# All products of y in 32-wide tiles, and the products for the carried state behind them in the same slot

## The chip, the cores and the metric

The kernel runs on one core of one Trainium2 chip. The metric is the device time of one execution in microseconds (us); lower is better. Engines are named as the profile names them: PE does the matmuls, PEld loads their weights, DVE, ACT and POOL do the elementwise work, SP issues the DMAs.

## The reference

Three stages follow one another: a gated linear attention over 4 batches of 8 heads, 768 positions and 48 features, then two MLPs over the 3072 tokens.

```
f = 1 / (1 + exp(-f_logit))
for t in range(S):
    state = f[:, :, t, :, None] * state + einsum('bhd,bhe->bhde', k[t], v[t])
    y[t]  = einsum('bhd,bhde->bhe', q[t], state)
x = y as (3072, 384)
x = (h * cos(h)) @ w_out,  h = x @ w_in                      # 384 -> 2048 -> 384
x = rmsnorm(x); out = (silu(x @ w_gate) * (x @ w_val)) @ w_out2
```

## The kernel before

**Steps and pieces.** The attention is done in 24 steps, each of which is one chunk of 128 positions of one batch (6 steps to a batch) and all 8 heads. Heads stand in 4 pairs i, with the two heads j of a pair at partitions 0 and 64. Within a step the product of q and k is masked and multiplied with v (the part inside the chunk), and q is multiplied with the state that the chunks before left (the carried part; the first step of a batch has none). A step's PE work is written in four pieces, `piece_pe(n, p)`:

- p = 0: transposes of the scaled k (`tr`), line 350 (not in the last step of a batch)
- p = 1: products of k and q for the two heads of each pair (`sc`), line 359
- p = 2: `zs(n)`, line 382: the products of k and v that are added to the carried state, 8 matmuls 64 columns wide with 48 columns moving (not in the last step of a batch)
- p = 3: `ys(n)`: the products that make y, in one PSUM bank of 128 x 384. For each of two groups c of heads there are two 64-wide matmuls of the carried state `Tz` with q (line 400) and four 32-wide ones of v with the masked product `am` (line 406). They cover 32 of the 48 features of each head. The 16 others follow 32 wide: four with `Tz` (line 412) and eight with the tile `vtl` (line 418).

Each of these calls is an fp32 matmul, and the trace shows each as two matmuls, so that line 382 has 16 in a step. "Wide" is the number of columns of weights, and so of output partitions; narrow matmuls that write different partitions can run beside each other.

**Slots.** Steps 0 to 3 run in a prologue (`PROLOGUE`). From then on the pieces are dealt out one to a slot, and a slot is one tile of 128 of the first MLP's 2048 hidden features for one block of 512 tokens: there are 6 blocks of 16 slots. On PE a slot is `H` (9 matmuls, line 606), then the piece `P`, then `m1_out` of the slot two before (9 matmuls, line 657). The string `SLOT` (first block, middle blocks, last block) gives the order in which the engines' instructions are written; every engine works through its own in that order. What DVE, ACT and POOL do for a piece is written one slot later, in the slot whose `p0` is that piece's number:

- p0 = 0: `kn` (ACT copies the transposed k out of PSUM), `ff`, `grd` and `scan` (the gates of the next step: a scan on DVE whose end values POOL copies to `pall`)
- p0 = 1: `am` (mask of the product), second `scan`
- p0 = 2: `st` (`state`, line 462: DVE adds the products of `zs` to the state), `kt` (k of the next step scaled)
- p0 = 3: `xh` and `xl` (y split into two parts by ACT and DVE), `qt` (q of the next step scaled), `cy` (`carry`, lines 325 and 331: the state times the chunk's decay, on DVE and into `Tz` on POOL)

For the MLP each slot has `k` (ACT, line 615), `w` (DVE, line 621), `s` (ACT, line 627), `g` (DVE, line 632), and for the slot before it `hi` (ACT, line 640) and `lo` (POOL, line 647, tile `gl`). On POOL, the copy to `pall` is written ahead of `lo`. In the third slot of a block ACT also empties the three accumulators of the block before (line 669), and `m1_out` waits for it; that slot always holds a piece p = 3 (steps 8, 12, 16 and 20).

**Banks.** From step 4 on the PSUM banks of the pieces come in turn from three (`att_bank`): `tr` one, `sc` two, `zs` one, `ys` one. `FLIP` is 10: up to step 9 PE transposes f, k and q of the next step behind the pieces (`turn1`, line 231), from step 10 on DVE does it.

Of the kernel before, what the change touches and what calls it, by code (L numbers as in the profile page):

```python
# [28 lines left out]

SLOT = (  # L30
# [3 lines left out]
)  # L34
SLOT2 = (
# [14 lines left out]
def kernel(  # L50
# [14 lines left out]
    nc = tc.nc  # L65
    B, H, S, D = q.shape
# [3 lines left out]
    C = 128  # L70
# [48 lines left out]
    xh = [pp.tile([128, KD, 512], F32R, name=f"xh{i}") for i in range(2)]  # L119
    xl = [pp.tile([128, KD, 512], F32R, name=f"xl{i}") for i in range(2)]  # L120
# [4 lines left out]
    FLIP = 10  # L125
# [4 lines left out]
    am = [ap_.tile([128, 512], F32, name=f"am{i}") for i in range(2)]  # L130
    vtl = [ap_.tile([128, NP, 3, 16], F32, name=f"vtl{i}") for i in range(2)]
# [38 lines left out]
    st = {}  # L170
# [174 lines left out]
    def piece_pe(n, p):  # L345
        if p == 0:
            if not last(n):
                t = st[n, "tr"] = att_bank()
                for i in range(NP):
                    nc.tensor.transpose(t[:, 128 * i:128 * (i + 1)], st[n, "kt"][:, i, :], ident)  # L350
            if n >= HEAD and n + 1 < NSTEP:
                turn1(n + 1, 0)
                load_v(n + 1)
        elif p == 1:
            t = [att_bank(), att_bank()]
            for i in range(NP):
                for j in range(2):
                    o = 64 * j
                    nc.tensor.matmul(  # L359
                        t[j][:, C * i:C * (i + 1)], st[n, "kt"][o:o + D, i, :],  # L360
                        st[n, "qt"][o:o + D, i, :], start=True, stop=True,
                    )
            st.pop((n, "kt"))
            st[n, "sc"] = t
        elif p == 2:
            zs(n)
            if n >= HEAD and n + 1 < NSTEP:
                turn1(n + 1, 1)
        else:
            ys(n)  # L370
            if n >= HEAD and n + 1 < NSTEP:
                turn1(n + 1, 2)

    def zs(n):
        if last(n):
            return
        t = att_bank()
        kn = st.pop((n, "kn"))
        for i in range(NP):
            for j in range(2):  # L380
                o = 64 * j
                nc.tensor.matmul(
                    t[o:o + 64, D * i:D * (i + 1)], kn[:, 128 * i + o:128 * i + o + 64],
                    st[n, "v"][:, 2 * i + j, :], start=True, stop=True,
                )
        st[n, "z"] = t

    def ys(n):
        if True:
            t = att_bank()  # L390
            qt, vt, vt2 = st.pop((n, "qt")), st.pop((n, "v")), vtl[n % 2]
            inter = n % NCH > 0


            for c in range(2):
                cs = slice(C * c, C * (c + 1))
                if inter:
                    for x in range(2):
                        i = 2 * c + x
                        nc.tensor.matmul(  # L400
                            t[64 * x:64 * x + 64, cs], Tz[:, i, 0:64], qt[:, i, :],
                            start=True, stop=False,
                        )
                for x in range(4):
                    i, j = divmod(4 * c + x, 2)
                    nc.tensor.matmul(  # L406
                        t[32 * x:32 * x + 32, cs], vt[:, 2 * i + j, 0:32],
                        am[j][:, C * i:C * (i + 1)], start=not inter, stop=True,
                    )
            if inter:  # L410
                for i in range(NP):
                    nc.tensor.matmul(
                        t[32 * i:32 * i + 32, 2 * C:3 * C], Tz[:, i, 64:96], qt[:, i, :],
                        start=True, stop=False,
                    )
            for j in range(2):
                for i in range(NP):
                    nc.tensor.matmul(  # L418
                        t[32 * i:32 * i + 32, 2 * C:3 * C], vt2[:, i, j:j + 2, :],
                        am[j][:, C * i:C * (i + 1)],  # L420
                        start=not inter and j == 0, stop=j == 1,
                    )
            st[n, "y"] = t
# [413 lines left out]
    if True:  # L837
# [120 lines left out]
        for j, (t0, N) in enumerate(blocks):  # L958
            final = j == len(blocks) - 1
            if final:  # L960
                assert not pieces and prev is None
                att.close()
                p2 = stack2.enter_context(tc.tile_pool(name="p2", bufs=1))
                for x in range(4):
                    free2.append(tuple(
                        p2.tile([128, DM], F32R, name=f"xunit{2 * x + y}") for y in range(2)
                    ))
                for i in range(N1):
                    free2 += [wi[i], wo[i]]
                order2 = [(nm, i) for i in range(N2) for nm in ("g", "v", "o")]  # L970
                for u, key in enumerate(order2):
                    w2[key] = free2[u]
                dec2 = Decode([
                    (w_out2_w, 128 * i, None, lambda nm=nm, i=i: w2[nm, i]) if nm == "o"
                    else (w_gate_w if nm == "g" else w_val_w, None, 128 * i,
                          lambda nm=nm, i=i: w2[nm, i])
                    for nm, i in order2
                ], 1)
                norm(0, slot + 8)
            for i in range(N1):  # L980
                cur = pieces.pop(0) if pieces else None
                n0, p0 = prev or (0, -1)
                more = n0 + 1 < NSTEP
                env = dict(d=dec if j == 0 else dec2)
                do = {
                    "H": lambda: m1_h(j, i),
                    "pe": lambda: run(pe_at, slot),
                    "hi": lambda: gp and m1_hi(*gp),
                    "lo": lambda: gp and m1_lo(*gp),
                    "kn": lambda: p0 == 0 and not last(n0) and kn_evac(n0),  # L990
                    "tanh": lambda: p0 == 0 and n0 + 1 < FLIP and gates(n0 + 1),
                    "ff": lambda: p0 == 0 and more and flip_f(n0 + 1),
                    "grd": lambda: p0 == 0 and more and (
                        guard_f(n0 + 1), n0 + 1 >= FLIP and gates(n0 + 1)
                    ),
                    "scan": lambda: more and (
                        p0 == 0 and scan_end(n0 + 1) or p0 == 1 and scan_start(n0 + 1)
                    ),
                    "am": lambda: p0 == 1 and causal(n0),
                    "st": lambda: p0 == 2 and state(n0),  # L1000
                    "kt": lambda: p0 == 2 and more and scale_k(n0 + 1),
                    "qt": lambda: p0 == 3 and more and scale_q(n0 + 1),
                    "xh": lambda: p0 == 3 and x_hi(n0),
                    "xl": lambda: p0 == 3 and x_lo(n0),
                    "cy": lambda: p0 == 3 and more and carry(n0 + 1),
                    "act": lambda: run(act_at, slot),
                    "k": lambda: env.update(k=m1_k(j, i)),
                    "w": lambda: env.update(w=m1_w(j, i, env["k"])),
                    "s": lambda: m1_cos(j, i, env["w"]),
                    "dv": lambda: run(dve_at, slot),  # L1010
                    "g": lambda: env.update(g=m1_g(j, i, env["w"])),
                    "t": lambda: env["d"] and env["d"].step_split(),
                    "x": lambda: env["d"] and env["d"].step_x(),
                    "f": lambda: env["d"] and env["d"].step_f(),
                    "po": lambda: run(post_at, slot),
                    "P": lambda: cur and piece_pe(*cur),
                }
                for key in SLOT[0 if j == 0 else 2 if final else 1].split():
                    do[key]()
                gp = j, i, env["g"]  # L1020
                prev = cur
                outs.append((j, i))
                if len(outs) > 2:
                    m1_out(*outs.pop(0))
                slot += 1
            finish(j, slot, final)
# [285 lines left out]
```

## Time and profile before

| | |
|---|---|
| median of 3 runs | 1039.61 us (1038.75 to 1039.67) |
| the profiled execution | 1038.93 us, of which the trace spans 1037.2 us |
| PE busy in the span | 996.0 us (96%) |
| DVE, ACT, POOL busy | 622.0 us (60%), 418.9 us (40%), 324.4 us (31%) |
| instructions | 15616, 5920 of them matmuls |

Times of the trace are counted from the start of the span. A matmul's row gives its start and a modelled duration; matmuls overlap, so the distance from one start to the next says what one costs.

### The profile page before, as it was taken

The numbers are of one execution on the slowest core, as the hardware profiler recorded it, in microseconds if no ns is written. First come the engines' busy times: TensorE is split into PE (matmuls) and PEld (weight loads), VectorE is DVE, ScalarE is ACT, GpSimd is POOL, SyncE is SP. The second block draws the span as 40 slices with busy tenths as digits, with TensorE's granted clock in tenths as the row PEclk, the third lists the DMA queues.
The fourth block names the chain that finished last, engine by engine and source line by source line (L and its number), as shares of the span: only waits on it lengthen the run. The fifth ranks groups of instructions, "written<-read, shape, count | busy, mean of one in ns | idle before, by whom it ended". The sixth has DMA issues, their size and how long they took to land.

```text
span 1037.2 us, 15616 instructions
## 1 busy us (share of the span) xinstructions
PE 996.0 (96%) x5920; PEld 812.7 (78%) x5920; DVE 622.0 (60%) x946; ACT 418.9 (40%) x737; POOL 324.4 (31%) x374
## 2 busy tenths in 40 slices
PE   6788899999999999999999999999999999999997
PEld 5556677777777777777777788888888888888886
DVE  7888875777777777776478676335335335335222
ACT  2466655444445444453677544212212222222111
POOL 1555653532532444344388353001001001001000
PEclk9799999999999999999999999999999999999999
DMA  8875222222223222321243443342343343332000
GB/s 172 193 186 134 80 59 71 60 50 66 80 65 71 81 56 59 93 46 9 91 132 93 145 148 107 92 132 87 112 132 92 110 141 95 122 117 61 31 1 34
DMA packets 123855, 96.10 MB, mean 93 GB/s; under 512 B 69238, under 2 KB 103030, under 8 KB 123772
## 3 DMA queue, kind: packets, MB, share of 16 engines
q1 hardware_dynamic: 123772, 95.03, 33.8%
q8 instruction: 48, 0.79, 0.3%
q14 instruction: 35, 0.29, 0.1%
HBM read 85.54 MB, written 9.46 MB: 92 GB/s over the span
## 4 chain that ended last, share of the span: by engine, by line
PE 80%; DVE 9%; ACT 4%; issue 2%; DMA 2%; POOL 2%; SPq 1%; DVEq 0%; ACTq 0%; POOLq 0%
PE bank L759 29%; PE bank L657 16%; PE bank L795 15%; PE bank L606 13%; DVE E L284 1%; PE bank L359 1%; PE bank L406 1%; DVE wrap L621 1%; PE bank L400 1%; DVE g L632 1%; PE bank L418 1%; DVE wx L562 1%; DMA nat<-in_k_dram 1%; DVE ft L293 1%; ACT wrap L627 1%
## 5 line engine op out<-in xcount | busy, mean ns | idle before, releaser
L657 PE MATMUL bank<-gh,wo 128*128 128x512 f32 x576 | 207.4, 414 | 4.4 <-ACT x L669 4.3
L773 DVE SCALAR_TENSOR_TENSOR u<-bank,sg 128x512 f32<-128x512 f32 x72 | 49.7, 691 | 199.4 <-PE bank L759 199.4
L647 POOL TENSOR_TENSOR gl<-g,gh 128x512 fp32r<-128x512 f32 x96 | 126.6, 1319 | 87.6 <-ACT gh L640 86.4
L657 PEld LDWEIGHTS bank<-gh,wo 128*128 128x128 f32 x576 | 109.2, 190 | 34.0 <-ACT x L669 5.4
L759 PE MATMUL bank<-xh,wo 128*128 128x512 f32 x360 | 122.8, 395 | 0.0
L657 PE MATMUL bank<-gl,wo 128*128 128x512 f32 x288 | 115.8, 402 | 6.5 <-POOL gl L647 6.4
L768 ACT ACTIVATE sg<-bank 128x512 f32<-128x512 f32 x72 | 43.0, 597 | 173.3 <-PE bank L759 173.3
L743 POOL TENSOR_TENSOR xl<-x2b,xh 128x512 fp32r<-128x512 f32 x18 | 24.2, 1344 | 283.1 <-ACT xh L742 283.1
L780 ACT CAST uh<-u 128x512 fp32r<-128x512 f32 x72 | 44.8, 622 | 151.1 <-DVE u L773 150.9
L627 ACT ACTIVATE wrap<-wrap,cb 128x512 f32<-128x512 f32 x96 | 69.3, 722 | 88.1 <-DVE wrap L621 87.4
L640 ACT CAST gh<-g 128x512 fp32r<-128x512 f32 x96 | 59.6, 620 | 106.4 <-DVE g L632 71.9
L632 DVE SCALAR_TENSOR_TENSOR g<-bank,wrap 128x512 f32<-128x512 f32 x96 | 65.6, 683 | 43.3 <-ACT wrap L627 41.5
L621 DVE SCALAR_TENSOR_TENSOR wrap<-bank,kint 128x512 f32<-128x512 f32 x96 | 65.8, 685 | 35.1 <-ACT kint L615 34.5
L615 ACT ACTIVATE kint<-bank,cb 128x512 int32<-128x512 f32 x96 | 65.9, 686 | 43.6 <-PE bank L606 43.3
L786 DVE TENSOR_TENSOR ul<-u,uh 128x512 fp32r<-128x512 f32 x72 | 51.5, 716 | 48.9 <-ACT uh L780 48.9
L759 PEld LDWEIGHTS bank<-xh,wo 128*128 128x128 f32 x360 | 67.6, 188 | 14.6
L795 PE MATMUL bank<-wo,uh 128*128 128x384 f32 x288 | 74.1, 338 | 0.0
L657 PEld LDWEIGHTS bank<-gl,wo 128*128 128x128 f32 x288 | 54.7, 190 | 21.4 <-POOL gl L647 10.2
L759 PE MATMUL bank<-xl,wo 128*128 128x512 f32 x180 | 71.0, 394 | 0.0
L795 PEld LDWEIGHTS bank<-wo,uh 128*128 128x128 f32 x288 | 52.7, 188 | 3.5 <-issue 0.5
L581 POOL TENSOR_TENSOR wo<-wx,wo 128x384 fp32r<-128x384 f32 x32 | 36.0, 1124 | 52.4 <-ACT wo L580 50.1
L490 DVE SCALAR_TENSOR_TENSOR wacc<-stage,wacc 128x384 int32<-128x384 int32 x68 | 50.8, 748 | 0.7
(343 smaller groups left out, 2196.9 us busy)
## 6 DMA issues: line engine op xcount, KB each, us to landing
stage<-in_moe_w_out_dram SPq DMA_DIRECT2D x56, 384.0 KB, 3.3
stage<-in_moe_w_gate_dram SPq DMA_DIRECT2D x24, 384.0 KB, 3.3
stage<-in_moe_w_val_dram SPq DMA_DIRECT2D x24, 384.0 KB, 3.3
stage<-in_moe_w_in_dram SPq DMA_DIRECT2D x16, 384.0 KB, 3.4
nat<-in_f_logit_dram SPq DMA_DIRECT2D x48, 96.0 KB, 2.2
nat<-in_k_dram SPq DMA_DIRECT2D x48, 96.0 KB, 2.3
nat<-in_q_dram SPq DMA_DIRECT2D x48, 96.0 KB, 2.2
v_sb<-in_v_dram SPq DMA_DIRECT2D x24, 192.0 KB, 3.6
```

What stands on the lines that cost most here:

```text
L490: nc.vector.scalar_tensor_tensor(out=wacc, in0=hi, scalar=1 << 30, in1=wacc, op0=ALU.bitwise_xor, op1=ALU.bitwise_and,)
L606: nc.tensor.matmul(t, l[:, 128 * kk:128 * (kk + 1)], r[:, kk, 0:N], start=idx == 0, stop=idx == 3 * KD - 1,)
L615: nc.scalar.activation(out=kt, in_=hb[j, i], func=AF.Identity, scale=INV2PI * UNIT, bias=cb[:, 0:1])
L621: nc.vector.scalar_tensor_tensor(out=w, in0=hb[j, i], scalar=INV2PI * UNIT, in1=kt, op0=ALU.mult, op1=ALU.subtract)
L627: nc.scalar.activation(out=w, in_=w, func=AF.Sin, scale=2.0 * math.pi, bias=cb[:, 1:2])
L632: nc.vector.scalar_tensor_tensor(out=g, in0=hb.pop((j, i)), scalar=UNIT, in1=w, op0=ALU.mult, op1=ALU.mult)
L640: nc.scalar.copy(out=h, in_=g)
L647: nc.gpsimd.tensor_tensor(out=l, in0=g, in1=h.bitcast(F32), op=ALU.subtract)
L657: nc.tensor.matmul(acc[m][:, 0:N], lw[:, cs], r, start=i == 0 and x == 0, stop=i == N1 - 1 and x == 2,)
L759: nc.tensor.matmul(t[y], l[:, 128 * kk:128 * (kk + 1)], r[:, kk, :], start=idx == 0, stop=idx == 3 * KD - 1,)
L786: nc.vector.tensor_tensor(out=l, in0=u, in1=h.bitcast(F32), op=ALU.subtract)
L795: nc.tensor.matmul(o2[tt][:, 0:DM], lu[:, cs], r, start=i == 0 and x == 0, stop=i == N2 - 1 and x == 2,)
```

## The change

In `ys`, the 64-wide matmuls with `Tz` become twice as many 32-wide ones, so that all of `ys` is 32 wide. For the steps from 9 on, `zs` moves from piece 2 to piece 3, behind `ys`, and is made of 16 matmuls 32 wide in place of 8 that are 64 wide; `state` moves with it to the slot whose `p0` is 3. In the second string of `SLOT`, `st` is written ahead of `kt`, `xh`, `xl`, `qt` and `cy`.

```
-    "tanh hi H kn ff kt xh xl qt cy am st P k w grd scan s lo act dv g pe po",
+    "tanh hi H kn ff st kt xh xl qt cy am P k w grd scan s lo act dv g pe po",
...
         elif p == 2:
-            zs(n)
+            if n + 1 < FLIP:
+                zs(n)
             if n >= HEAD and n + 1 < NSTEP:
                 turn1(n + 1, 1)
         else:
             ys(n)
+            if n + 1 >= FLIP:
+                zs(n)
...
+        M = 64 if n + 1 < FLIP else 32
         for i in range(NP):
-            for j in range(2):
-                o = 64 * j
+            for o in range(0, 128, M):
                 nc.tensor.matmul(
-                    t[o:o + 64, D * i:D * (i + 1)], kn[:, 128 * i + o:128 * i + o + 64],
-                    st[n, "v"][:, 2 * i + j, :], start=True, stop=True,
+                    t[o:o + M, D * i:D * (i + 1)], kn[:, 128 * i + o:128 * i + o + M],
+                    st[n, "v"][:, 2 * i + o // 64, :], start=True, stop=True,
                 )
...
             for c in range(2):
                 cs = slice(C * c, C * (c + 1))
-                if inter:
-                    for x in range(2):
-                        i = 2 * c + x
+                for part in (0, 1) if inter else (1,):
+                    for x in range(4):
+                        i, j = divmod(4 * c + x, 2)
                         nc.tensor.matmul(
-                            t[64 * x:64 * x + 64, cs], Tz[:, i, 0:64], qt[:, i, :],
-                            start=True, stop=False,
+                            t[32 * x:32 * x + 32, cs],
+                            vt[:, 2 * i + j, 0:32] if part else Tz[:, i, 32 * j:32 * j + 32],
+                            am[j][:, C * i:C * (i + 1)] if part else qt[:, i, :],
+                            start=part == 0 or not inter, stop=part == 1,
                         )
-                for x in range(4):
-                    i, j = divmod(4 * c + x, 2)
-                    nc.tensor.matmul(
-                        t[32 * x:32 * x + 32, cs], vt[:, 2 * i + j, 0:32],
-                        am[j][:, C * i:C * (i + 1)], start=not inter, stop=True,
-                    )
...
-                    "st": lambda: p0 == 2 and state(n0),
+                    "st": lambda: p0 >= 2 and state(n0),
```

## Rows read from the trace of the kernel before

**Rows 1.** The page: busy time, share of the span and instructions of each engine.

```profile
PE 996.0 (96%) x5920; PEld 812.7 (78%) x5920; DVE 622.0 (60%) x946; ACT 418.9 (40%) x737; POOL 324.4 (31%) x374
```

**Rows 2.** PE's waits from 160 to 500 us: total us, times, longest.

```profile
PE bank L657 <- ACT x L669: 4.3, 3, 2.0
```

**Rows 3.** Windows, one slot each: length; PE, PEld, DVE, ACT, POOL busy (instructions); clock; DMA.

```profile
226.33:230.70 4.37, 4.37 (x20) 3.30 (x19) 4.26 (x8) 1.68 (x3) 2.98 (x4) 1.00 0.13 17
488.79:492.96 4.17, 4.17 (x19) 3.38 (x18) 1.99 (x4) 1.70 (x3) 1.29 (x1) 1.00 0.44 21
315.04:320.00 4.96, 4.96 (x36) 3.85 (x34) 4.85 (x8) 1.93 (x3) 2.97 (x4) 1.00 0.03 1
320.00:326.48 6.48, 6.48 (x68) 4.67 (x66) 4.84 (x7) 2.03 (x3) 2.65 (x5) 1.00 0.28 58
```

**Rows 4.** Timeline of PE across `ys` of step 14: start, length, line, count.

```profile
300.67 0.44 PE L400 MATMUL bank<-qt,Tz 128*64 128x128 f32 x4
301.04 0.43 PE L406 MATMUL bank<-am,v_sb 128*32 128x128 f32 x8
301.40 0.44 PE L400 MATMUL bank<-qt,Tz 128*64 128x128 f32 x4
...
302.01 0.40 PE L412 MATMUL bank<-qt,Tz 128*32 128x128 f32 x8
302.23 0.62 PE L418 MATMUL bank<-am,vtl 128*32 128x128 f32 x16
302.78 0.50 PE L657 MATMUL bank<-gh,wo 128*128 128x512 f32 x1
```

**Rows 5.** `zs` of step 14 by line: duration ns min/median/max, first and last start.

```profile
L382 PE MATMUL bank<-v_sb,kn x16: 222/222/257, 295.7 to 296.1; 128*64 128x48 f32 x16
```

**Rows 6.** Timeline of DVE after `ys` of step 14.

```profile
306.21 0.56 DVE L438 TENSOR_TENSOR xl<-bank,xh 128x384 fp32r<-128x384 f32 x1 [2.23 <-ACT xh L433]
```

**Rows 7.** Timeline, slots with piece 2 of steps 11 and 15.

```profile
227.38 1.29 POOL L647 TENSOR_TENSOR gl<-g,gh 128x512 fp32r<-128x512 f32 x1
...
228.40 0.40 PE L657 MATMUL bank<-gh,wo 128*128 128x512 f32 x1
...
314.71 1.23 DVE L284 TENSOR_TENSOR_SCAN E<-ft,c 128x516 f32<-128x516 f32 x1
...
316.16 1.29 POOL L647 TENSOR_TENSOR gl<-g,gh 128x512 fp32r<-128x512 f32 x1
...
317.80 0.50 PE L657 MATMUL bank<-gh,wo 128*128 128x512 f32 x1
```

**Rows 8.** Timeline, third slot of a block (piece 3 of step 16).

```profile
344.77 0.34 DVE L462 TENSOR_TENSOR Sn<-Sn,bank 128x192 f32<-128x192 f32 x1
...
345.03 0.67 DVE L621 SCALAR_TENSOR_TENSOR wrap<-bank,kint 128x512 f32<-128x512 f32 x1
...
346.37 1.06 ACT L669 ACTIVATE x<-bank 128x512 f32<-128x512 f32 x2
...
347.00 0.50 PE L657 MATMUL bank<-gh,wo 128*128 128x512 f32 x1 [1.17 <-ACT x L669]
```

**Rows 9.** Windows right after that slot of step 12, and in the prologue.

```profile
258.10:261.50 3.40, 3.40 (x10) 2.64 (x9) 0.00 (x0) 0.65 (x2) 0.00 (x0) 0.50 0.59 231
...
26.00:32.80 6.80, 4.25 (x51) 2.74 (x52) 6.16 (x14) 1.11 (x2) 4.08 (x6) 0.50 0.85 185
```

**Rows 10.** The chain that ended last, in order of time, in the prologue.

```profile
28.55 0.69 PE bank L400 x4
...
45.49 1.25 PE bank L406 x8
```

**Rows 11.** PE's own queue: waits it passed, by line (`ys` of step 6; step 14).

```profile
117.54 0.64 PE L406 MATMUL bank<-am,v_sb 128*32 128x128 f32 x16
...
L231 PEldq EVENT_SEMAPHORE  x1: 51/51/51, 117.8 to 117.8; - x1
...
L382 PEldq EVENT_SEMAPHORE  x1: 51/51/51, 291.5 to 291.5; - x1
```

More of the change, by code (lines that the diff above doesn't have):

```diff
@@ L390, in ys @@
             t = att_bank()
-            qt, vt, vt2 = st.pop((n, "qt")), st.pop((n, "v")), vtl[n % 2]
+            qt, vt, vt2 = st.pop((n, "qt")), st[n, "v"], vtl[n % 2]
             inter = n % NCH > 0
```

## The prediction

> **What bounds the kernel now.** I read the page first: PE is busy for 996 of the span's 1037.2 us [rows 1]. That share alone says little, since a busy PE can be waiting inside a matmul, so I went on to PE's waits. From 160 us on, where steps 8 to 23 run, almost all that PE waits for is the emptying of the accumulators, 4.3 us in three slots [rows 2]; until then the first block's slots are ended by waits on DVE, ACT and POOL. Then I cut the middle blocks into slots. A slot without a piece takes 4.17 us; one with piece 2 takes 4.96, one with piece 3 takes 6.48, and PE is busy in all of each [rows 3]. The two pieces thus cost 0.79 and 2.31 us, and what they lose the kernel loses, as long as nobody else comes late.
>
> **Part 1: all of `ys` 32 wide.** I read `ys` of step 14 by the starts of its groups [rows 4]. Four 32-wide matmuls run side by side: in the middle of a 32-wide stretch 8 matmuls, two groups of four, take 302.23 - 302.01 = 0.22 us, 0.109 a group. A 64-wide stretch, two groups of two, takes 0.37 (300.67 to 301.04), and the 32-wide stretch between two 64-wide ones takes 0.36 for its two groups, so that 0.36 - 0.22 = 0.14 is the price of beginning and ending a stretch. Now: 2.11 us from 300.67 to 302.78, in four stretches. After: 14 groups in one stretch, 14 x 0.109 + 0.14 = 1.67. The gain is 0.44 us for a step with a carried part. The 4 more matmuls (8 in the trace) that the step gets are in the 14 groups already.
>
> **Part 2: `zs` behind `ys`.** Its slot falls back from 4.96 to 4.17, a gain of 0.79 [rows 3]. In the slot of `ys` come 32 matmuls, 8 groups of four with 48 columns moving. No row has such a group. The nearest are 0.109 for 128 columns [rows 4], of which 48 columns are in proportion 0.041, and the 64-wide `zs`, whose eight pairs start between 295.7 and 296.1, 0.06 from pair to pair [rows 5]. Bounds for the addition: 8 x 0.03 = 0.25 (half the pair's, if the loading of weights sets it) and 8 x 0.109 = 0.87 (if the columns don't count). I take 0.041 and a little for the step from long to short groups, 0.35. The beginning and the end of a stretch are paid by `ys` already. A full step, one with both parts, gains 0.44 + 0.79 - 0.35 = 0.88.
>
> **Part 3: `state` moves.** DVE did it between `kt` and `w` of the slot of `ys`; now it comes before `xl` in the next slot, where DVE stands idle for 2.23 us until ACT has done `xh` [rows 6]. It costs nothing there, and `cy`, which needs it, is written after it. `Tz` follows on POOL some 3 us later than now, and its reader is the `ys` four slots on. No DMA is moved. The banks change their turn, `ys` before `zs`, but each is taken where its former reader is done two slots earlier.
>
> **What comes late next.** The slot of piece 2 now runs `m1_out` sooner after `H`: 2.07 us after the slot's start, as in step 11's (226.33 to 228.40), in place of 2.76 (315.04 to 317.80) [rows 3, 7]. `m1_out` there needs `gl` of two slots before, and POOL does that after the copy to `pall`, which waits for the DVE scan that ends at 315.94: `gl` lands at 317.45, now 0.35 us ahead of its use [rows 7]. That chain starts at the end of the slot of `ys` and runs through ACT and DVE without PE, so it doesn't shorten. With 0.69 less it comes 0.34 late. Step 11, which has no `zs`, shows the price: its `gl` lands 0.27 after the use [rows 7] and its slot takes 4.37 in place of 4.17, 0.20 longer [rows 3]. So the stall is the lateness less 0.07. I read the same lead in all twelve steps with a moved `zs`; 0.35 is typical (steps 13, 15, 16, 19, 20), 0.6 in 9 and 12, 0.09 in 21, over 1.1 in 10, 14, 18 and 22. Stalls: 0.24, 0.26 and 0.28 in 13, 15 and 19, 0.52 in 21, 0.02 in 9, together 1.32 us.
>
> **Where the gain is lost.** In the third slot of a block PE stands until ACT empties the accumulators: 1.17 us in step 16 [rows 8], 2.0 in the longest [rows 2]. What sets that moment in steps 12, 16 and 20 is DVE's order `kt`, `st`, `w`, then ACT. The shorter PE work before it only lengthens the wait; the kernel gains what `st` took between 344.77 and 345.03, 0.27 us [rows 8]. In step 8, whose wait follows `H`, nothing is gained.
>
> **The sum.** Full steps (9, 10, 13, 14, 15, 19, 21, 22): 8 x 0.88 - 1.32 = 5.72. Step 18, without a carried part: 0.79 - 0.35 = 0.44. Steps 7, 11, 17 and 23, `ys` alone: 4 x 0.44 = 1.76. Steps 12, 16 and 20: 3 x 0.27 = 0.81. Steps 4 to 6 lie where others end the slots: 0. In the prologue, `ys` of steps 1 and 3 is on the chain that ended last [rows 10], at a granted clock of 0.50 [rows 9], but DVE and DMA waits follow; between 0 and 0.9 for both I take 0.4. Together 9.1 us. The profiled execution took 1038.93, 0.68 under the median, so 1029.8 on its scale and **1030.5 us** on the median's.
>
> **The rivals.**
>
> *A. Each narrow matmul has a price of its own, whatever its columns.* No row shows one cheaper than 0.027 us (8 in 0.22 [rows 4]); 32 of these are 0.87. The addition grows by 0.52 in the eight full steps and step 18: 4.7 us less gain, 1035.2. Against: a pair of `zs` with 48 columns takes 0.06 [rows 5] where a group with 128 takes 0.109 [rows 4], so columns do count. The Trainium skill ("TensorE: Matmul & The Clock Gate", Back-to-back issue gap) states an issue floor of about 25 ns for 1 to 64 columns; by it the addition would be an estimated 0.8 us and the time about 1034.6; no row here shows a matmul alone on its columns at that rate.
>
> *B. The chain to `gl` loses its lead everywhere.* If DVE's chain lengthens by some tenths (POOL's later `Tz` is the only new thing on it), all nine free steps stall by 0.6: 9 x 0.6 - 1.32 = 4.1 less, 1034.6. Against: nothing is added to it.
>
> *C. The granted clock.* After step 12's wait the clock is 0.50 for 3.4 us [rows 9], at half speed, some 1.7 lost. The waits of steps 16 and 20 grow by about 0.2 and didn't do that so far; if both do now, 3.4 more: 1033.9. If step 12's no longer does, 1028.8.
>
> *D. Slower: PE is not fed fast enough.* A merged stretch has 56 + 32 = 88 matmuls in 2.02 us. PE's queue passed the wait in front of `zs` of step 14 at 291.5, 4.2 us before it ran [rows 11, 5], about 17 matmuls of 0.23. So 71 must be handed over within the stretch; the full step's gain is gone at (2.02 + 0.88) / 71 = 0.041 us each. With the 0.051 that a wait takes in that queue [rows 11], a merged stretch takes 71 x 0.051 = 3.62, a full step loses 0.72, step 18 0.6, and `ys` alone gains 0.1. With the stalls of 1.32 still there and the 0.8 and 0.4 of the waits and the prologue, that is 6.0 us more than before, 1045.6. Against: `ys` of step 6 starts at 117.54 and the queue has passed the wait behind its 32 matmuls at 117.8 [rows 11]; with 17 ahead that is 15 in 0.26, 0.017 each. The Trainium skill (same page and section) names 62 ns per matmul where the sequencer's microcode decodes them; by it the time would be near 1053 by estimate, and the 0.017 speaks against it.
>
> *E. The waits, not the widths, cost the time*, and nothing moves: within 2 us. Against: the starts of [rows 4] repeat in the 14 other such steps from step 7 on, to 0.01 us, whatever the other engines do then.
>
> **How the numbers follow.** Forecast 0.60 (its own range 1027.5 to 1033), A 0.14, B 0.07, C's worse half 0.06, D 0.07, E 0.06 (0.04 of it within 0.2%, 0.02 slower by another way). 0.2% is 2.1 us, about what a measurement of this kernel can tell from no change. Faster: forecast, A, B and C, 0.87; same 0.04; slower 0.09. The range takes in C's better half with the cheap bound of `zs` (9 x 0.1) and the prologue's 0.9 below, and A with the prologue's 0 above: 1026.5 to 1036.
>
> **What would show it.** `ys` of a step with a carried part in 1.67 us in one stretch of 32-wide groups, 0.109 apart; `zs` right behind it, 0.35 long; slots of piece 2 at 4.2 to 4.5 with the excess ended by `gl`; slots of piece 3 at 6.4; the wait for the accumulators in steps 16 and 20 at 1.2 to 1.5. I am wrong if the groups of `zs` stand 0.1 apart (A), if PE has gaps inside the stretch that no semaphore ends (D), or if the slots of piece 2 stay near 4.9 (B).

## The result and the profile after

The changed kernel takes 1031.34 us (median of 6 runs, 1030.31 to 1031.79) against 1039.3 for the kernel before (6 runs): a ratio of 0.9917 (0.9906 to 0.9928), 8.0 us faster. The forecast was 1030.5, 9.1 us faster on its scale. The profiled execution took 1030.7, with a span of 1029.0. Line numbers have shifted: `zs` is now L385, the two loops of `ys` that were L400 and L406 are one call, L403, and its last matmuls are L411 and L417; from there on every line has moved up by one, so that `m1_out` is L656, `H` L605 and `gl` L646.

The first row of the page of the kernel after: PE has 352 matmuls more than in [rows 1] and is busy for 11 us less; DVE and POOL are busy for nearly as long as before.

```profile
PE 985.0 (96%) x6272; PEld 815.6 (79%) x6272; DVE 623.7 (61%) x946; ACT 418.8 (41%) x737; POOL 327.7 (32%) x374
```

Timeline of PE, kernel after, `ys` and `zs` of step 14, which answers to [rows 4, 5]:

```profile
296.06 0.43 PE L403 MATMUL bank<-qt,Tz 128*32 128x128 f32 x8
296.31 0.40 PE L403 MATMUL bank<-am,v_sb 128*32 128x128 f32 x8
296.52 0.40 PE L403 MATMUL bank<-qt,Tz 128*32 128x128 f32 x8
296.74 0.40 PE L403 MATMUL bank<-am,v_sb 128*32 128x128 f32 x8
296.96 0.40 PE L411 MATMUL bank<-qt,Tz 128*32 128x128 f32 x8
297.18 0.62 PE L417 MATMUL bank<-am,vtl 128*32 128x128 f32 x16
297.62 0.52 PE L385 MATMUL bank<-v_sb,kn 128*32 128x48 f32 x32
298.07 0.50 PE L656 MATMUL bank<-gh,wo 128*128 128x512 f32 x1
```

Two groups of four still take 0.22 us, from one row to the next, and no stretch is broken. From the start of `ys` to `m1_out` it is 298.07 - 296.06 = 2.01 us; the working gave 1.67 + 0.35 = 2.02. `zs` with all its 32 matmuls takes 0.45 from its start to the next piece of work, the stretch's end included.

Windows of the kernel after, one slot each (columns as in [rows 3]): piece 2 of steps 11, 23, 14, 15 and 19, piece 3 of steps 14 and 15, and the third slot of a block, steps 12 and 16:

```profile
225.21:229.59 4.38, 4.38 (x20) 3.30 (x19) 4.26 (x8) 1.67 (x3) 2.98 (x4) 1.00 0.15 18
481.09:485.26 4.17, 4.17 (x20) 3.38 (x18) 2.00 (x4) 1.71 (x3) 1.30 (x1) 1.00 0.70 31
289.75:293.91 4.16, 4.16 (x20) 3.38 (x19) 3.88 (x8) 1.77 (x3) 2.98 (x4) 1.00 0.00 0
310.30:314.75 4.45, 4.43 (x19) 3.30 (x18) 4.34 (x8) 1.66 (x3) 2.98 (x4) 1.00 0.05 1
395.20:400.19 4.99, 4.44 (x20) 3.30 (x19) 4.83 (x9) 2.02 (x4) 2.96 (x4) 1.00 0.15 20
293.91:300.26 6.35, 6.35 (x108) 5.24 (x106) 5.36 (x7) 2.30 (x4) 1.29 (x2) 1.00 0.29 59
314.75:321.92 7.17, 6.62 (x108) 5.40 (x106) 5.38 (x7) 2.30 (x4) 2.03 (x3) 1.00 0.25 53
249.81:257.77 7.96, 5.76 (x84) 4.58 (x82) 5.39 (x7) 3.75 (x7) 2.65 (x5) 1.00 0.24 66
...
336.41:344.37 7.96, 6.45 (x108) 5.24 (x107) 5.38 (x7) 3.76 (x7) 2.66 (x5) 1.00 0.23 62
```

A slot of piece 2 in which PE waits for nobody (a free slot) is down from 4.96 to 4.16; step 15's takes 4.45, and step 19's takes 4.99, no less than before the change. Piece 3 is down from 6.48 to 6.35 in step 14 but up to 7.17 in step 15. What PE waited for from 160 to 500 us (total us, times, longest), to be set beside [rows 2]:

```profile
PE bank L656 <- ACT x L668: 5.8, 4, 2.2
PE bank L656 <- POOL gl L646: 1.1, 3, 0.6
PE bank L385 <- issue: 0.5, 1, 0.5
```

In the kernel before, the same view has a second row for `gl`:

```profile
PE bank L657 <- POOL gl L647: 0.2, 1, 0.2
```

Three things took gain back, and each has a row: the accumulators (5.8 us against 4.3), `gl` (1.1 against 0.2), and once an empty PE with no semaphore to end the wait, in `zs` of step 15 (timeline, kernel after):

```profile
318.45 0.46 PE L385 MATMUL bank<-v_sb,kn 128*32 128x48 f32 x25
319.46 0.33 PE L385 MATMUL bank<-v_sb,kn 128*32 128x48 f32 x7 [0.55 <-issue]
319.71 0.50 PE L656 MATMUL bank<-gh,wo 128*128 128x512 f32 x1
```

**Step by step.** From the starts of the slots in the two traces, the change of each step's time (its slots of piece 2 and 3 and the two that follow): 10, 14 and 22, -0.93 each; 9, -0.93; 13, -0.41; 15, +0.19; 19, -0.13; 21, -0.38; 18, -0.46; 11 and 23, -0.45; 17, -0.71; 16 and 20, -0.29 and -0.27; 8, 0.00; 12, -1.82. Together -8.89 from step 8 to the end of the attention, for which the prediction's terms give 5.72 + 0.44 + 3 x 0.44 + 0.81 = 8.29. But that stretch begins at 150.58 in place of 149.84, 0.74 later, where 0.84 earlier was forecast (0.4 for the prologue, 0.44 for step 7). 8.89 less 0.74 is what the rest of the program starts sooner, 8.16 us by the unrounded times.

### The profile page after: what moved, and what is told of

It is laid out like the page before. It is cut to its first block, busy times and chain, and to the rows that moved or that the text cites. A ratio compares the mean times of both kernels' runs of the same rounds, so it can differ in the third digit from the quotient of the medians.

```text
span 1029.0 us, 16308 instructions
## 1 busy us (share of the span) xinstructions
PE 985.0 (96%) x6272; PEld 815.6 (79%) x6272; DVE 623.7 (61%) x946; ACT 418.8 (41%) x737; POOL 327.7 (32%) x374
## 4 chain that ended last, share of the span: by engine, by line
PE 75%; DVE 9%; ACT 5%; DMA 3%; SPq 3%; issue 3%; POOL 2%; DVEq 0%; ACTq 0%; POOLq 0%
PE bank L758 29%; PE bank L794 15%; PE bank L656 14%; PE bank L605 12%; DVE wrap L620 1%; DVE E L284 1%; PE bank L403 1%; DVE g L631 1%; SPq L189 1%; PE bank L359 1%; DMA nat<-in_k_dram 1%; SPq L477 1%; ACT wrap L626 1%; POOL gl L646 1%; ACT kint L614 1%
## 5 line engine op out<-in xcount | busy, mean ns | idle before, releaser
L656 PE MATMUL bank<-gh,wo 128*128 128x512 f32 x576 | 206.6, 413 | 5.8 <-ACT x L668 5.8
L646 POOL TENSOR_TENSOR gl<-g,gh 128x512 fp32r<-128x512 f32 x96 | 126.7, 1320 | 63.3 <-ACT gh L639 61.8
L656 PEld LDWEIGHTS bank<-gh,wo 128*128 128x128 f32 x576 | 110.0, 191 | 33.3 <-ACT x L668 6.4
L656 PE MATMUL bank<-gl,wo 128*128 128x512 f32 x288 | 116.8, 406 | 6.2 <-POOL gl L646 6.0
L656 PEld LDWEIGHTS bank<-gl,wo 128*128 128x128 f32 x288 | 55.1, 191 | 24.5 <-POOL gl L646 13.0
```

The source lines that it names most:

```text
L646: nc.gpsimd.tensor_tensor(out=l, in0=g, in1=h.bitcast(F32), op=ALU.subtract)
L656: nc.tensor.matmul(acc[m][:, 0:N], lw[:, cs], r, start=i == 0 and x == 0, stop=i == N1 - 1 and x == 2,)
```

## The experiments

**Halves of the change.** In this section the `-` lines are those of the kernel after, if nothing else is said. First the narrow `ys` alone:

```diff
         elif p == 2:
-            if n + 1 < FLIP:
-                zs(n)
+            zs(n)
...
             ys(n)
-            if n + 1 >= FLIP:
-                zs(n)
```

(`zs` 64 wide, `st` and `p0 == 2` as before.)

> The matmuls of y all 32 wide, everything of zs and state as before. If PE's stretches cost what the rows say, 0.44 us goes in each of the twelve steps 7, 9 to 11, 13 to 15, 17, 19 and 21 to 23; steps 8, 16 and 20 lose it to the wait for the accumulators: 5.3 us faster than before. If the narrow ys is what cost some 1.1 us in the prologue and the first block of the changed kernel's profile, only about 4.2 us. If the widths cost nothing (rival E), within 1 us of before.

Measured: 1032.75, ratio 0.9941 (0.9925 to 0.9958), 6.1 us by the ratio, where 5.3 were expected. Slots of piece 3 take 6.03 in place of 6.48, 0.45 less, and free slots of piece 2 stay at 4.96: no new stall for `gl` arises. Step 12, in which this half changes nothing, gains 1.56 in the profile: the granted clock stays at 1.00 behind its wait, where it fell in the kernel before [rows 9]. Then the other half, the moved narrow `zs` with `ys` as before:

```diff
-                for part in (0, 1) if inter else (1,):
-                    for x in range(4):
-                        i, j = divmod(4 * c + x, 2)
+                if inter:
+                    for x in range(2):
+                        i = 2 * c + x
                         nc.tensor.matmul(
-                            t[32 * x:32 * x + 32, cs],
...
+                            t[64 * x:64 * x + 64, cs], Tz[:, i, 0:64], qt[:, i, :],
```

> zs 32 wide behind ys and state one slot later, ys itself as before. The slots of piece 2 fall back to 4.2 us, the slots of ys grow by 0.31: 0.48 in nine steps is 4.3 us, less stalls for gl of 2.2 (steps 13, 15, 19, 21), plus 0.8 in steps 12, 16 and 20, plus 1.6 if the granted clock stays up after step 12: 2.9 to 4.5 us faster than before. If the move gains only together with the narrow ys, within 1 us of before.

Measured: 1036.6, ratio 0.9974 (0.9963 to 0.9984), 2.7 us (2.9 to 4.5 were expected). The free slots of piece 2 fall to 4.16 to 4.19, piece 3 rises from 6.48 to 6.79, by 0.31, and PE waits 2.0 us for `gl`, as expected. In the slots the halves add up: 0.45 and 0.78 - 0.31 = 0.47 make 0.92 for a full step, where the change gains 0.93, and the new stalls for `gl` come from the moved `zs` alone. That 6.1 and 2.7 make 8.8 against the change's 8.6 by the ratio says less: the two intervals are 1.7 and 1.1 us wide to either side, and in the profiles the clock that stays up in step 12 is in both halves, but only once in the change.

**The stalls for `gl`.** On POOL, `lo`, which makes `gl`, goes ahead of the copy to `pall`:

```diff
-    "tanh hi H kn ff st kt xh xl qt cy am P k w grd scan s lo act dv g pe po",
+    "tanh hi H kn ff st kt xh xl qt cy am P k w grd lo scan s act dv g pe po",
```

> The changed kernel with lo written ahead of scan, so that on POOL gl no longer stands behind the copy to pall. If the chain through DVE's scan ends the slots of piece 2, the stalls there go (0.2 in step 11, 0.52 in 13, 0.28 in 15, 0.19 in 17, 0.81 in 19, 0.55 in 21): 2.5 us less than the changed kernel, 10.5 less than before. If another thing holds m1_out there, the time stays that of the changed kernel, 8.0 less than before.

Measured: 1033.49, ratio 0.9941 (0.9927 to 0.9955), 6.1 us: not 2.5 us faster than the change, as expected, but by the ratios 2.5 us slower (its interval begins where the change's ends). The stalls are gone; in the profile every slot of piece 2 takes 4.16 to 4.19, 3.1 us less in sum. PE's waits from 160 to 500 us in this kernel:

```profile
PE bank L656 <- ACT x L668: 7.5, 4, 2.8
PE bank L385 <- issue: 0.9, 1, 0.9
PE bank L683 <- ACT kn L426: 0.5, 1, 0.5
```

PE reaches the third slot of a block sooner and waits longer there. In two of them (steps 12 and 20) the granted clock falls to 0.50, the lower of its two levels (1.2 in place of 2.4 GHz), for 3.4 us; windows of this kernel (columns as above), the slot of step 12 and the fallen stretch within it:

```profile
248.99:258.50 9.51, 7.19 (x84) 5.65 (x83) 5.53 (x7) 3.89 (x7) 3.55 (x6) 0.82 0.36 115
254.60:258.00 3.40, 3.11 (x7) 2.49 (x8) 0.81 (x2) 1.21 (x3) 1.38 (x4) 0.50 0.40 152
```

That slot is 1.54 longer than in the kernel after by the unrounded times (9.51 against 7.96), and step 20's by 2.31. In this profile what the stalls gave back is spent at the next wait.

**The first steps.** `ys` of steps 1 to 6 as before the change (only the head of the edit is shown):

```diff
-            for c in range(2):
-                cs = slice(C * c, C * (c + 1))
-                for part in (0, 1) if inter else (1,):
+            if n < 7:
+                for c in range(2):
...
+            else:
+                for c in range(2):
```

> The changed kernel, but ys of steps 1 to 6 with its 64-wide matmuls as before. If the narrow ys in the prologue and the first block is what made the profile of the changed kernel 0.7 us late at step 8, where 0.8 less was forecast, it is now about 1.1 us faster than the changed kernel, 9.1 less than before. If that lateness comes from when DMAs land and differs from run to run, the time is that of the changed kernel within 0.5 us; if the forecast 0.4 of the prologue is real, 0.4 slower.

Measured: 1032.16, ratio 0.9927 (0.9912 to 0.9941), 7.6 us, not to be told from the change's 8.6 by the ratio. The first slot of step 8's turn begins at 152.60 in its profile. Over the profiles of all kernels of this document it begins at 149.84, 150.91, 152.60 and 151.42 where these `ys` have their 64-wide matmuls, and at 149.06 to 150.58 (eight profiles) where they are 32 wide. The means are 151.2 and 149.7. So the 0.74 by which the change's profile is late lies within the scatter of the first 150 us, and so does the forecast 0.84 earlier: single profiles don't resolve it. The means speak rather for more than for less, but the experiment doesn't show it.

**Narrow or wide `zs` behind `ys`.**

```diff
-        M = 64 if n + 1 < FLIP else 32
+        M = 64
```

> The changed kernel, but the moved zs keeps its 64-wide matmuls, so that one more stretch begins and ends in the slot of ys. By the rows a 64-wide zs is a stretch of 0.60 where the 32-wide one adds 0.31: 0.29 more in nine steps, 2.6 us more than the changed kernel, 5.4 less than before. If only the place counts and not the width, the time is that of the changed kernel, 8 less than before.

Measured: 1033.78, ratio 0.9949 (0.9931 to 0.9968), 5.3 us (5.4 were expected). PE's timeline of this kernel, step 14:

```profile
297.94 0.62 PE L417 MATMUL bank<-am,vtl 128*32 128x128 f32 x16
298.49 0.67 PE L385 MATMUL bank<-v_sb,kn 128*64 128x48 f32 x16
299.10 0.50 PE L656 MATMUL bank<-gh,wo 128*128 128x512 f32 x1
```

From L417 to `m1_out` it is 1.16 us in place of 298.07 - 297.18 = 0.89, 0.27 more a step. 0.11 of it stands ahead of `zs`, where the stretch breaks again (0.55 from L417 to L385 in place of 0.44); 0.16 is in `zs` itself, whose eight pairs and the end of the stretch take 0.61 in place of 0.45. The move alone thus pays 0.78 - 0.31 - 0.27 = 0.20 a step, and the width that `zs` shares with `ys` pays the larger part.

**What limits the narrow matmuls.** Every product of `zs` behind `ys` is computed twice, the second time over the first one's output:

```diff
-        for i in range(NP):
+        for i in [y for y in range(NP) for _ in range(1 if n + 1 < FLIP else 2)]:
```

> The changed kernel with each moved product of zs computed twice, the second time over the first (64 matmuls in the trace in place of 32). By the stretch's own cadence, 0.041 us for a group of four, 0.33 more in nine steps: 3.0 us more than the changed kernel, 5.0 less than before; the other three steps hide it in the wait for the accumulators. If PE's queue is near the limit of what it is handed (rival D), the further 32 come at 0.05 each: 14 us more, slower than before.

Measured: 1033.6, ratio 0.9936 (0.9919 to 0.9954), 6.7 us, 2.0 less than the change by the ratio, where 3.0 less were expected from the columns and 14 from a PE that is not fed fast enough. PE's timeline of this kernel, step 14:

```profile
298.29 0.62 PE L417 MATMUL bank<-am,vtl 128*32 128x128 f32 x16
298.73 0.86 PE L385 MATMUL bank<-v_sb,kn 128*32 128x48 f32 x64
299.52 0.50 PE L656 MATMUL bank<-gh,wo 128*128 128x512 f32 x1
```

64 matmuls take 0.79 where 32 take 0.45: 0.34 for 32 more, 0.042 a group of four, 0.011 a matmul. 120 narrow matmuls in a row cause no gap in PE. The Trainium skill ("TensorE: Matmul & The Clock Gate", Back-to-back issue gap) gives an issue floor of about 25 ns a matmul for 1 to 64 columns. For four tiles side by side this run does not agree, and the measured 11 ns decides.

**Both waits taken away.** Besides `lo`, the emptying of the accumulators (`act`) is written ahead of `k`, in the kernel after and, as a second run, in the kernel before:

```diff
-    "tanh hi H kn ff st kt xh xl qt cy am P k w grd scan s lo act dv g pe po",
+    "tanh hi H kn ff st kt xh xl qt cy am P act k w grd lo scan s dv g pe po",
```

> The changed kernel with two reorderings of what is written: lo ahead of scan, and act, the emptying of the accumulators, ahead of k, so that ACT does it while PE is still at H. If the waits for gl (2.5 us) and for the accumulators in steps 8, 12, 16 and 20 (0.8, 2.3, 1.6 and 1.6) are all that the change loses, 8.8 us less than the changed kernel: 16.8 less than before. If ACT and DVE are then late at the next place, as with lo alone, half of it: 12 less than before.

> The kernel before with the same two reorderings. Its waits for the accumulators (0.35, 2.05, 1.2, 1.2), the half clock after step 12 (1.6) and the stalls in steps 11 and 17 (0.65) go: 7 us less than before. The changed kernel with the same reorderings should then lie 10 to 12 us below this one, more than the 8 that the change gains with the waits in place, since these hid 0.9 us in steps 16 and 20 and 0.45 in 8 and 12.

Measured: the kernel after with these orders 1028.06, ratio 0.9883 (0.9865 to 0.9901), 12.2 us, the smaller of the two numbers expected; the kernel before with them 1033.91, ratio 0.994 (0.9924 to 0.9956), 6.2 us where 7 were expected. The two lie 6.0 us apart, not 10 to 12 as expected: the waits taken away, the change gains less than with them. In the profiles, the second has no wait of PE left between 160 and 500 us. The first has one kind, new:

```profile
PE bank L683 <- ACT kn L426: 5.6, 3, 2.3
```

L683 is the matmul that sums the squares for rmsnorm, in the slot of piece 1 of steps 14, 18 and 22; its bank is one that ACT still reads (`kn`). With PE this far ahead that reader is late, and in step 22 the granted clock falls to 0.50 as well (from 454.65, for 3.4 us). So the sum goes into the next slot, with what follows it:

```diff
-            at(pe_at, s + 8, lambda: set_((j, "r"), m1_sum, j, held.pop((j, "x2"))))
-            at(post_at, s + 9, lambda: m1_put(j, held.pop((j, "r"))))
+            at(pe_at, s + 9, lambda: set_((j, "r"), m1_sum, j, held.pop((j, "x2"))))
+            at(post_at, s + 10, lambda: m1_put(j, held.pop((j, "r"))))
```

> The kernel with both waits taken away, and the matmul that sums the squares of a block one slot later (a slot of piece 2, where the bank that it takes is long free). If that bank, held by the transposes until ACT has copied them, is all that PE waited for there (2.0, 1.5 and 3.9 us in three slots), 7.4 us less than without it: 1020.7, 18.8 less than before. If DVE and ACT as a whole have become the limit, PE waits as long at the next place and the time stays near 1028.

Measured: 1025.39, ratio 0.9854 (0.9838 to 0.9871), 15.2 us, the lowest median of all versions and by the ratios 9.0 us less than the kernel before with the same orders. The waits for `kn` are gone. What is missing to the expected 18.8 stands in its profile mostly in one place: PE stands still in `H` behind step 15, and the granted clock is 0.50 for 3.4 us from the end of this gap on (319.52). Timeline of this kernel:

```profile
316.92 0.39 PE L605 MATMUL bank<-xh,wi15h 128*128 128x512 f32 x1
...
319.64 0.63 PE L605 MATMUL bank<-xh,wi15l 128*128 128x512 f32 x1 [2.33 <-issue]
```

That slot takes 8.65 in place of 4.59. Last, `act` alone written ahead of `k`, with `lo` and the sum where they were:

```diff
-    "tanh hi H kn ff st kt xh xl qt cy am P k w grd scan s lo act dv g pe po",
+    "tanh hi H kn ff st kt xh xl qt cy am P act k w grd scan s lo dv g pe po",
```

> The changed kernel with act ahead of k alone; lo stays behind scan, so that the stalls for gl stay. If the waits for the accumulators in steps 8, 12, 16 and 20 (0.8, 2.3, 1.6 and 1.6 us) go and nothing else moves, 6.3 us less than the changed kernel, 14.3 less than before, and so less time than with lo moved as well, since there PE ran ahead into the wait at the sum. If DVE and ACT are late elsewhere, some 11 less than before.

Measured: 1026.58, ratio 0.9868 (0.9848 to 0.9887), 13.7 us, not to be told from the version before it; 14.3 were expected if nothing else moved. But something did. Its waits from 160 to 500 us:

```profile
PE bank L656 <- POOL gl L646: 3.8, 4, 1.5
PE bank L385 <- issue: 0.6, 1, 0.6
```

The stalls for `gl` grow (3.8 us in place of 1.1), and PE never waits for the sum's bank; that the one keeps it from the other is likely, not shown.

## Why the prediction was right

**The mechanism, `ys`: as forecast.** 0.44 a step was worked out; steps 11 and 23, which have only this, gain 0.45.

**`zs`: as forecast, and rival A falls.** 0.79 was forecast for its old slot and 0.78 seen; 0.35 for the new one and 0.31 seen (6.79 against 6.48 with `ys` unchanged). `state` does lie in DVE's idle time, as forecast: behind step 14 DVE still stands idle for 1.32 us ahead of `xl`. A's 0.87 was the upper bound; groups of 48 columns take 0.042, those of 128 columns 0.109, so columns count. A full step gains 0.93 where nothing stalls (0.88 forecast), and step 18 gains 0.46 (0.44).

**Steps 8, 16, 20: as forecast.** The wait swallows all but what DVE no longer does ahead of `w`: 0.29 and 0.27 against 0.27, and nothing in step 8. The wait of step 16 is 1.51, where 1.2 to 1.5 were forecast. The kernel with `act` ahead of `k` shows what the wait hides: there the slots of steps 16 and 20 take 6.37 in place of 7.95.

**The term that was mis-sized: the stalls for `gl`.** The prediction put them at 1.32; the excess over a free slot is 0.52 in step 13, 0.28 in 15, 0.81 in 19 and 0.55 in 21, 2.16 in all. Steps 15 and 21 are right (0.26 and 0.52). The lead was taken from the trace of before as if DVE's chain kept its place against PE, and in two steps, 13 and 19, it didn't:

- Step 13: before, the clock of 0.50 reached into the slot behind step 12 [rows 9], 4.94 in place of 4.60. With that 0.34 gone, PE is 0.34 earlier and the chain is not: 0.24 + 0.34 = 0.58 against 0.52 seen. Two experiments bear it out: with `zs` twice and with the first steps wide the clock fell there, that slot took 4.90 and 5.29, and the stall of step 13 is 0.27 and 0.16.
- Step 19: timelines behind step 18, the `gh` that starts the turn and the multiplication that makes `qt`, first in the kernel before, then in the kernel after:

```profile
391.34 0.62 ACT L640 CAST gh<-g 128x512 fp32r<-128x512 f32 x1 [0.89 <-PE bank L657]
...
393.99 0.69 DVE L314 TENSOR_TENSOR qt<-qt,ft 128x512 f32<-128x512 f32 x1
```

```profile
385.53 0.62 ACT L639 CAST gh<-g 128x512 fp32r<-128x512 f32 x1 [0.88 <-DVE g L631]
...
388.19 1.06 DVE L314 TENSOR_TENSOR qt<-qt,ft 128x512 f32<-128x512 f32 x1
388.78 0.52 POOL L700 TENSOR_SCALAR ssc<-ssc 128x4 f32<-128x4 f32 x1
```

Step 18 has no carried part and its slot is short (5.71), so PE comes to its end ahead of DVE: `gh` waits for DVE there and no longer for PE, starts 0.38 after the slot that follows (385.15) in place of 0.20 (391.14 in the kernel before), and the multiplication takes 0.37 longer. (POOL's L700 overlaps it; behind step 14 of the kernel after it does so too, and the multiplication takes 0.69 there, so why it takes longer stays open.) 0.35 + 0.18 + 0.37 = 0.90 late, less 0.07 by the prediction's rule 0.83; the slot lost 0.81. The runs in which step 18's slot is longer agree: with `zs` 64 wide and twice it takes 5.96 and 6.05, `gh` waits for PE again, the multiplication takes 1.00 and 0.93, and step 19 stalls by 0.60 and 0.50, where the same sum gives 0.59 and 0.52. The kernel with `zs` moved alone shows the same long slot as the change (5.01). How lateness comes to a stall is to be read in the trace of the kernel after:

```profile
395.44 1.23 DVE L284 TENSOR_TENSOR_SCAN E<-ft,c 128x516 f32<-128x516 f32 x1
...
396.88 1.28 POOL L646 TENSOR_TENSOR gl<-g,gh 128x512 fp32r<-128x512 f32 x1
...
397.27 0.40 PE L656 MATMUL bank<-gh,wo 128*128 128x512 f32 x1
...
398.22 0.50 PE L656 MATMUL bank<-gl,wo 128*128 128x512 f32 x1 [0.55 <-POOL gl L646]
```

`gl` begins when the scan and the copy behind it are done and ends at 398.16; PE, which began `m1_out` at 397.27, has stood idle for 0.55 when it goes on at 398.22.

**Rival D, small and once.** Step 15 loses 0.81 to a gap that no semaphore ends. It is not the rate at which narrow matmuls are handed over: with `zs` doubled, 120 of them run without a gap. What stands beside the gap is told in the last section; its cause stays open.

**Rival C's better half came true, and as far as the runs show that was luck.** Step 12 gains 1.82 in place of 0.27, since the clock does not fall behind its wait; with it 1.55 of the 8.89 is not the change's doing as forecast. The prediction gave no reason why the clock should stay up, and the wait there became longer, not shorter (2.20 against 1.98). In the kernel with the first steps wide, which from step 7 on is the kernel after and waits 2.19 there, the clock falls again, as it does with `zs` 64 wide or twice behind `ys`, where the slot takes 9.38 and 9.19.

**The sum again.** Steps 8 to 23: 8.29 forecast, less 0.84 for the stalls, less 0.81 for the gap, plus 1.55 for the clock, plus 0.39 for full steps worth 0.93, plus 0.25 for step 17, where a stall for `gl` became shorter, and 0.06 in the others: 8.89, as seen. The errors cancelled each other, and that the total came so close is luck as well; the median's 8.0 does not tell them apart, the slots do. Rivals B (all nine free steps stalling by 0.6) and E fall by the same windows.

**Where the rest of the gain lies.** The kernel before without its waits takes 342.5 us from step 8's turn to the end of the attention, the version with the sum one slot later 335.9, although 4.06 of these are its one gap: without the waits the narrow stretches are worth 342.5 - 335.9 + 4.06 = 10.7 there, by one profile of each. In the change as made it is 8.89, or 8.15 without the clock's 1.55 and the gap's 0.81.

## What to carry to other kernels

Put narrow matmuls of one width behind each other: a change of width had a price here (0.14 us for the 32-wide stretch between two 64-wide ones), and short products at the end of a long stretch cost little more than their columns. On an engine that is the bound, read for each stage which wait ends last: the gain is paid out only in stages that wait for nobody, and a lead read in the old trace holds only while the other engines keep their place against the bound one. Taking away a single wait can lose time, when the engine then waits longer at the next one: here the shorter wait (`gl`) taken away alone lost 2.5 us against the change, the longer one (the accumulators) alone gained 5. And read a total slot by slot before calling it explained: two errors that cancel look like a hit.

## What the runs showed of the hardware

**A gap in PE beside a long instruction transfer.** In the windows of the DMA queues, the transfer of instructions (queue, packets, MB, share of 16 engines' time) near step 15's gap, first the kernel after, from 316 to 322 us, then the doubled `zs`, same window:

```profile
q8 instruction: 1, 0.02, 2.3%
```

```profile
q8 instruction: 1, 0.02, 3.7%
```

2.3% of 16 x 6 us is 2.2 us for one packet, 3.7% is 3.6; from 280 to 290 us in the kernel after one took 0.6%, 1.0 us. Such long transfers with a gap in PE beside them: the kernel after 2.2 us (gap 0.55), `lo` ahead 2.9 (0.9), `act` alone 2.6 (0.6), the sum later 3.7 (2.3; there the gap begins at 317.3, after the transfer has ended at 316.9). Without a gap: the doubled `zs` (3.6), both waits taken away (3.2), `zs` moved alone (3.3, from 317.35 on), and the run with the sum later once more, with 6.8 us from 231.73 on. So a long transfer stands beside each gap but doesn't suffice; whether it is the cause, and what else it takes, stays open, and no run here was made on it.

**The granted clock after a wait.** Eight kernels of this document have the wait for the accumulators in step 12. The clock fell to 0.50 (1.2 in place of 2.4 GHz) for 3.4 us at waits of 1.98 (the kernel before), 2.32 (`lo` ahead), 2.19 (first steps wide), 1.93 (`zs` 64 wide behind `ys`) and 1.84 (`zs` twice); it did not at 2.20 (the kernel after), 1.99 (narrow `ys` alone) and 2.17 (`zs` moved alone). With `lo` ahead it fell at 254.6, before the matmuls had begun again at 254.89. The length of the wait alone does not tell it.
